# The residual subtractions of a fused attention and MLP kernel: from VectorE or GpSimd to VectorE alone

## The chip, the cores and the metric

One core of a Trainium2 chip. The metric is the device time of one execution in microseconds, the median of the runs shown; three runs of the kernel before are known.

## The reference, cut to what matters

```python
def reference(**kwargs):
    attn_out = _attn_ref(x, a, B, C)                # gated linear attention, 4 x 8 heads, 768 steps, D 32, N 16
    x = attn_out.transpose(0, 2, 1, 3).reshape(3072, 256)
    xn = x / sqrt(mean(x * x) + 1e-6) * rms_g       # MLP 1, d_ff 1536
    g, val = xn @ w_gate, xn @ w_val
    x = (g * sigmoid(g) * val) @ w_out
    h = x @ w_in                                    # MLP 2, d_ff 2048
    return (h * clip(h + 3, 0, 6) / 6) @ w_out2
```

All of it is float32.

## The kernel before, in words

**Two halves for every product.** A matmul operand is split into a high half, rounded to a matmul format (`hi`), and the residual, value minus high half (`lo`). Each product is then three matmuls: high by high, low by high, high by low (`mm3`, its matmuls are all line 752). The residual is one subtraction of two SBUF tiles, and it is issued by `two` (line 248), which takes the engine as an argument. Line 248 also issues two small attention products, `bh` and `ch`. So the tiles written by line 248 are `w1l` and `w2l` (weights), `xl` (a block's input), `gl` (the gated hidden tile), `bh` and `ch`.

**The stages.** Attention works on 24 chunks of 128 positions. A visit to a pair of chunks makes, per chunk, a scan of the decays on VectorE (`L`, line 400), `bh` and `ch`, the scores, the decayed scores (`SM`, line 480), the masked state (`um`), the states (`V`, line 494), and its output. Four chunks make a token block of 512. MLP 1 ("A") runs over 6 blocks with 12 steps each, MLP 2 ("B") over 6 blocks with 16 steps each. The first two pairs of chunks and the block's normalisation come ahead of A; the other chunks and the normalisations of later blocks (`z`, `y`, then `xT`, line 648, then `xh` and `xl`) are woven into the A steps. The weights of MLP 1 are rebuilt in the course of block 0: ScalarE makes two parts, VectorE joins them (line 712), ScalarE or VectorE rounds (`w1h`), and line 248 makes `w1l`.

**A step.** In A: 12 matmuls make two hidden tiles `hps`, ScalarE gates one (`p`, line 785), VectorE multiplies by the other (line 793), ScalarE rounds (`gh`, line 800), line 248 makes `gl`, and 6 matmuls add to `acc`. In B: 6 matmuls, ScalarE (line 787), VectorE (line 795), `gh`, `gl`, 6 matmuls. That makes 72 steps of 18 and 96 steps of 12 matmuls of 512 columns, 2448 in all. The hidden tiles lie in 2 PSUM buffers in A (4 from the middle of the last block but one on, and in B); `p`, `gh` and `gl` have 3 buffers each.

**What sets the order.** Nothing is ordered by hand. Every operation is handed to a planner (`Plan.op`) with the engines that may run it and what it is thought to cost there. At build time `Plan.run` plays the kernel through, gives each operation to one engine, and emits all instructions in the order of its start times; on the chip each engine then works through its list in order. Where an operation has two engines, the planner takes the one that would be done first, with 600 ns (`BIAS`) held against VectorE. While GpSimd runs something, the planner charges VectorE with 0.45 of its time (`SHARE`). `either(n)` (lines 244 and 245) hands over such a pair. It serves `bh` and `ch`, the `xl` of the first half of block 0 (the other half's is VectorE's by its own line) and of all later blocks, `w1l`, `w2l` and `gl`. By the planner's numbers a 512-column subtraction is 604 ns on VectorE (`d1`) and 1313 ns on GpSimd (`g1`), 0.45 of which is 591 ns.

Of the kernel before, what the change touches and what calls it, by code (L numbers as in the profile page):

```python
# [186 lines left out]
def block_kernel(ctx, tc, comb, ablk, w1, w2, cst, out):  # L187
# [44 lines left out]
    def d1(n):  # L232
        return 72 + 1.04 * n
# [7 lines left out]
    def g1(n):  # L241
        return 110 + 2.35 * n

    def either(n):
        return {"DVE": d1(n), "POOL": g1(n)}

    def two(e, out, a, b, op):
        eng[e].tensor_tensor(out=out, in0=a, in1=b, op=op)  # L248
# [92 lines left out]
    def load(q):  # L341
# [71 lines left out]
        for i, k in enumerate((k0, k0 + 1)):  # L413
            P.op({"DVE": ds(512)}, lambda e, k=k: scan(e, k), r=[("eye", 0), Ls[i]], w=[Ls[i]],
                 boost=bst)
            P.op(either(128), lambda e, k=k: bh(e, k), r=[cbs[i], Ls[i]], w=[("bh", k)], boost=bst)
            P.op(either(64 if k < B else 128), lambda e, k=k: ch(e, k), r=[cbs[i], ("P", q)],
                 w=[("ch", k)], boost=bst)
# [138 lines left out]
    def norm_pair(q, b):  # L557
# [44 lines left out]
        def lo(e):  # L602
# [3 lines left out]
        x = [("xT", 0, k0, t) for t in range(2)]  # L606
        P.op({"ACT": a1(512), "DVE": d2(512)}, hi, r=x, w=[("x", b, q, 0)], boost=bst)
        P.op({"DVE": d1(512)} if q else either(512), lo, r=x + [("x", b, q, 0)],
             w=[("x", b, q, 1)], boost=bst)

# [377 lines left out]
```

## Time and profile before

| | us |
|---|---|
| median of 3 runs (lowest, highest) | 643.24 (642.71, 643.81) |
| the profiled execution, its own time | 643.43 |
| span of its instructions | 641.6 |
| PE busy | 608.3 (95%) |
| PEld busy | 491.9 (77%) |
| DVE busy | 311.2 (49%) |
| ACT busy | 293.9 (46%) |
| POOL busy | 282.1 (44%) |

PE is TensorE's matmul, PEld its weight load, DVE VectorE, ACT ScalarE, POOL GpSimd. The span runs from the first to the last instruction. Busy times of PE overlap because matmuls are pipelined, so a window in which PE is shown as busy throughout can still hold fewer matmuls than it could.

### The profile page before, as it was taken

To read this page: it belongs to the slowest core of one execution; us is meant where nothing else is said; L and a number is where in the kernel's file an instruction comes from. 1 tells how busy PE (TensorE), PEld (TensorE's weight loads), DVE (VectorE), ACT (ScalarE), POOL (GpSimd) and SP (SyncE) were. 2 spreads that over 40 slices of the span, in tenths; PEclk is the share of its full clock that TensorE was granted. 3 is DMA by queue.
4 is the path that set the end of the run, shared out by engine and by line. 5 is a ranking of instruction groups with operands and counts; after the bars stand their busy time and mean duration, and the time that the engine had idled before them with its cause. 6 is when DMAs were issued, how large, how long until landed. Compare 5 with 4: busy or idle time off the path is not lost.

```text
span 641.6 us, 10828 instructions
## 1 busy us (share of the span) xinstructions
PE 608.3 (95%) x4414; PEld 491.9 (77%) x4414; DVE 311.2 (49%) x474; ACT 293.9 (46%) x484; POOL 282.1 (44%) x245
## 2 busy tenths in 40 slices
PE   1689999999999999999999999999999999999997
PEld 0567777778777777777888878788788787888886
DVE  4589975771683366255666422422424224222223
ACT  1368743232323233335766344545454454545443
POOL 3255373353334235233544344545455454544443
PEclk9999999999999999999999999999999999999999
DMA  7977314300340220022433000000000000000000
GB/s 254 313 241 287 102 32 129 105 18 1 100 111 7 79 79 17 3 83 76 140 131 113 0 1 0 1 33 2 1 34 1 0 34 1 5 29 1 33 1 33
DMA packets 15817, 42.18 MB, mean 66 GB/s; under 512 B 2116, under 2 KB 5400, under 8 KB 15768
## 3 DMA queue, kind: packets, MB, share of 16 engines
q1 hardware_dynamic: 15064, 39.63, 19.3%
q10 hardware_dynamic: 704, 1.87, 0.8%
q8 instruction: 34, 0.56, 0.4%
q14 instruction: 15, 0.12, 0.1%
HBM read 38.14 MB, written 3.35 MB: 65 GB/s over the span
## 4 chain that ended last, share of the span: by engine, by line
PE 78%; DVE 11%; DMA 5%; issue 4%; SPq 1%; ACT 0%; POOL 0%; DVEq 0%; POOLq 0%
PE hps L752 43%; PE acc L752 31%; DMA rb<-rnd 2%; DVE p L793 1%; DVE z L551 1%; DVE xT L648 1%; PE sps L451 1%; PE sps L460 1%; DVE xl L248 1%; DVE xh L254 1%; DVE yT L712 1%; DMA pref<-ac 1%; PE sps L426 1%; DVE y L552 1%; DMA rnd<-y 1%
## 5 line engine op out<-in xcount | busy, mean ns | idle before, releaser
L248 POOL TENSOR_TENSOR gl<-p,gh 128x512 fp32r<-128x512 f32 x161 | 215.5, 1338 | 300.0 <-ACT gh L800 279.7
L800 ACT CAST gh<-p 128x512 fp32r<-128x512 f32 x168 | 104.7, 623 | 117.2 <-PE acc L752 115.2
L795 DVE SCALAR_TENSOR_TENSOR p<-p,hps 128x512 f32<-128x512 f32 x96 | 65.9, 687 | 175.9 <-ACT p L787 175.8
L787 ACT ACTIVATE p<-hps,half 128x512 f32<-128x512 f32 x96 | 66.0, 687 | 76.9 <-POOL gl L248 76.2
L752 PE MATMUL hps<-xh,w1h 128*128 128x512 f32 x288 | 91.2, 398 | 4.4 <-DVE p L793 3.7
L752 PE MATMUL hps<-xh,w1l 128*128 128x512 f32 x288 | 89.4, 392 | 0.0
L752 PE MATMUL hps<-xl,w1h 128*128 128x512 f32 x288 | 89.2, 391 | 0.0
L793 DVE TENSOR_TENSOR p<-p,hps 128x512 f32<-128x512 f32 x72 | 49.1, 681 | 64.7 <-PE hps L752 56.3
L785 ACT ACTIVATE p<-hps 128x512 f32<-128x512 f32 x72 | 43.0, 598 | 79.4 <-POOL gl L248 66.2
L752 PE MATMUL acc<-gh,w2h 128*128 128x512 f32 x192 | 74.7, 389 | 0.0
L752 PE MATMUL acc<-gl,w2h 128*128 128x512 f32 x192 | 74.7, 389 | 0.0
L752 PE MATMUL acc<-gh,w2l 128*128 128x512 f32 x192 | 74.7, 389 | 0.0
L752 PEld LDWEIGHTS hps<-xh,w1h 128*128 128x128 f32 x288 | 53.1, 190 | 19.2 <-DVE p L793 6.8
L752 PEld LDWEIGHTS hps<-xh,w1l 128*128 128x128 f32 x288 | 54.4, 189 | 11.7
L752 PEld LDWEIGHTS hps<-xl,w1h 128*128 128x128 f32 x288 | 54.4, 189 | 11.6
L752 PE MATMUL hps<-xh,w2h 128*128 128x512 f32 x192 | 59.7, 392 | 2.1 <-DVE p L795 2.1
L752 PE MATMUL hps<-xh,w2l 128*128 128x512 f32 x192 | 59.2, 389 | 0.0
L752 PE MATMUL hps<-xl,w2h 128*128 128x512 f32 x192 | 59.1, 389 | 0.0
L752 PE MATMUL acc<-gh,w1h 128*128 128x512 f32 x144 | 57.4, 399 | 0.9 <-issue 0.9
L752 PE MATMUL acc<-gh,w1l 128*128 128x512 f32 x144 | 56.1, 390 | 0.0
L752 PE MATMUL acc<-gl,w1h 128*128 128x512 f32 x144 | 56.1, 390 | 0.0
L752 PEld LDWEIGHTS hps<-xh,w2h 128*128 128x128 f32 x192 | 35.6, 188 | 11.3 <-DVE p L795 4.3
(98 smaller groups left out, 710.4 us busy)
## 6 DMA issues: line engine op xcount, KB each, us to landing
cb<-comb SPq DMA_DIRECT2D x10, 896.0 KB
raw<-w SPq DMA_DIRECT2D x16, 512.0 KB
L<-azero SPq DMA_DIRECT2D x22, 256.0 KB
yT<-w SPq DMA_DIRECT2D x6, 768.0 KB
rawx<-w SPq DMA_DIRECT2D x6, 768.0 KB
out<-yT SPq DMA_DIRECT2D x12, 256.0 KB
P<-pref SPq DMA_DIRECT2D x24, 64.0 KB
rb<-rnd SPq DMA_DIRECT2D x5, 256.0 KB
```

The lines of the kernel that those rows point to most:

```text
L248: eng[e].tensor_tensor(out=out, in0=a, in1=b, op=op)
L254: dve.tensor_copy(out, a)
L426: pe.matmul(out=o[64 * c:64 * c + 64, p], lhsT=cb[r, BN + c * SC:BN + (c + 1) * SC], rhs=cb[r, CP + c * CH:CP + (c + 1) * CH], start=True, ...
L451: pe.matmul(out=y[32 * g:32 * g + 32, 2 * t + c], rhs=SM[r, h], lhsT=cb[r, XX + D * h:XX + D * h + D], start=first, stop=True, skip_group_ ...
L460: pe.matmul(out=y[q:q + 64, p // 2 * 2 + c], lhsT=before(k, c)[r, :], rhs=T["ch", k][r, SC * c:SC * c + SC], start=False, stop=True, skip_ ...
L551: dve.tensor_tensor(out=z, in0=z, in1=y, op=ALU.mult)
L752: pe.matmul(out=o, lhsT=a, rhs=c, start=first and i == 0, stop=last and i == len(seq) - 1)
L785: act.activation(out=p[:, :n], in_=hid(hs[0])[:, :n], func=AF.Silu)
L787: act.activation(out=p[:, :n], in_=hid(hs[0])[:, :n], func=AF.Relu, scale=1.0 / 6.0, bias=half)
L793: dve.tensor_tensor(out=p, in0=p, in1=h, op=ALU.mult)
L795: dve.scalar_tensor_tensor(out=p, in0=p, scalar=1.0, in1=h, op0=ALU.min, op1=ALU.mult)
L800: act.copy(out=t[:, :n], in_=T["p", i][:, :n])
```

## The change

`either` names VectorE alone. All operations handed over through it therefore run on VectorE, GpSimd keeps only the fills and masks of the setup, and the planner makes a new order for all engines.

```diff
     def either(n):
-        return {"DVE": d1(n), "POOL": g1(n)}
+        return {"DVE": d1(n)}
```

## Rows read from the trace of the kernel before

**Rows 1.** Windows: us, busy us (instructions) by engine, clock, DMA share, GB/s.
```profile
37.00:97.00 60.00, 57.85 (x613) 45.32 (x613) 55.11 (x77) 38.91 (x62) 33.55 (x29) 1.00 0.47 160
...
100.00:300.00 200.00, 195.79 (x2000) 155.88 (x1999) 109.10 (x185) 65.05 (x120) 76.40 (x72) 1.00 0.20 60
...
364.00:641.60 277.60, 271.71 (x1193) 223.07 (x1191) 86.28 (x118) 133.93 (x207) 131.56 (x102) 1.00 0.03 12
```
**Rows 2.** The chain that ended last: start us, us, what.
```profile
444.12 2.72 PE acc L752 x12
```
**Rows 3.** Waits of PE: us in total, times, longest us.
```profile
PE hps L752 <- DVE p L793: 3.7, 7, 0.8
...
PE hps L752 <- DVE p L795: 2.1, 5, 0.7
```
**Rows 4.** POOL by form, window 37 to 97: busy us, mean ns, idle before.
```profile
L248 POOL TENSOR_TENSOR gl<-p,gh 128x512 fp32r<-128x512 f32 x11 | 16.8, 1531 | 19.2 <-ACT gh L800 13.8 <-DVE w1l L248 5.5
L248 POOL TENSOR_TENSOR w1l<-yT,w1h 128x768 fp32r<-128x768 f32 x3 | 6.5, 2151 | 1.8 <-ACT w1h L252 1.8
L248 POOL TENSOR_TENSOR bh<-cb,L 128x128 f32<-128x128 f32 x8 | 5.8, 729 | 5.9 <-DVE L L400 5.9
L248 POOL TENSOR_TENSOR ch<-cb,P 128x128 f32<-128x128 f32 x6 | 3.3, 574 | 0.0
L248 POOL TENSOR_TENSOR xl<-xT,xh 128x512 fp32r<-128x512 f32 x1 | 1.7, 1747 | 0.0
```
**Rows 5.** DVE by tile, whole span: count, least/median/most ns, first and last start.
```profile
L248 DVE TENSOR_TENSOR gl<-p,gh x7: 679/802/1705, 298.8 to 632.9; 128x512 fp32r<-128x512 f32 x7
L248 DVE TENSOR_TENSOR w1l<-yT,w1h x7: 929/950/1945, 39.5 to 81.3; 128x768 fp32r<-128x768 f32 x7
L551 DVE TENSOR_TENSOR z<-z,y x17: 160/293/1269, 26.8 to 278.2; 128x128 f32<-128x128 f32 x15, 128x2 f32<-128x2 f32 x2
L400 DVE TENSOR_TENSOR_SCAN L<-L,eye x24: 1193/1214/2893, 9.8 to 230.5; 128x512 f32<-128x512 f32 x24
L494 DVE SCALAR_TENSOR_TENSOR V<-V,P,um x36: 270/277/1342, 49.5 to 269.4; 128x64 f32<-128x64 f32 x36
L648 DVE SCALAR_TENSOR_TENSOR xT<-xT,gs,rb x10: 739/1040/1777, 84.4 to 286.3; 128x512 f32<-128x512 f32 x10
```
**Rows 6.** DVE by form, window 37 to 97, columns as in rows 4.
```profile
L400 DVE TENSOR_TENSOR_SCAN L<-L,eye 128x512 f32<-128x512 f32 x7 | 12.0, 1747 | 0.0
L248 DVE TENSOR_TENSOR w1l<-yT,w1h 128x768 fp32r<-128x768 f32 x7 | 7.6, 1090 | 0.0
L494 DVE SCALAR_TENSOR_TENSOR V<-V,P,um 128x64 f32<-128x64 f32 x11 | 5.0, 495 | 0.0
L648 DVE SCALAR_TENSOR_TENSOR xT<-xT,gs,rb 128x512 f32<-128x512 f32 x2 | 3.1, 1582 | 1.3 <-DMA rb<-rnd 1.3
L551 DVE TENSOR_TENSOR z<-z,y 128x128 f32<-128x128 f32 x3 | 1.9, 617 | 0.1
```
**Rows 7.** Timeline 17.7 to 24.4: start us, us, instruction [idle before].
```profile
17.80 2.34 DVE L400 TENSOR_TENSOR_SCAN L<-L,eye 128x512 f32<-128x512 f32 x2 [1.13 <-DMA L<-azero]
20.87 1.81 POOL L248 TENSOR_TENSOR w1l<-yT,w1h 128x768 fp32r<-128x768 f32 x1 [6.11 <-ACT w1h L252]
22.64 0.78 POOL L248 TENSOR_TENSOR bh<-cb,L 128x128 f32<-128x128 f32 x2
21.06 1.16 PE L426 MATMUL sps<-cb 32*64 32x128 f32 x32
23.51 0.68 PE L437 MATMUL sps<-cb,bh 64*32 64x64 f32 x32 [1.30 <-POOL bh L248]
```
**Rows 8.** Timeline 405 to 412, the change from one block of B to the next.
```profile
406.33 1.14 DVE L254 CAST xh<-yT 128x512 fp32r<-128x512 f32 x1 [0.41 <-PE hps L752]
407.57 1.60 DVE L248 TENSOR_TENSOR xl<-yT,xh 128x512 fp32r<-128x512 f32 x1
409.10 0.67 DVE L795 SCALAR_TENSOR_TENSOR p<-p,hps 128x512 f32<-128x512 f32 x1
409.08 0.39 PE L752 MATMUL acc<-gl,w2h 128*128 128x512 f32 x1
409.82 0.73 PE L752 MATMUL hps<-xh,w2h 128*128 128x512 f32 x2 [0.36 <-DVE p L795]
```

## The prediction

> **What bounds the kernel now.** I read the windows first, then the chain that ended last, then the waits of PE, and last the two engines that the change touches. The windows show three regimes [rows 1]. From 364 us to the end (MLP 2) PE is busy nearly all the time and VectorE for 86.28 of 277.6 us. The chain there is made of runs of matmuls such as 12 in 2.72 us [rows 2], that is 0.227 us each; the 2448 matmuls of the two MLPs at this pitch are 555 us of the 641.6 us span. No change on VectorE can shorten that part. From 100 to 300 us VectorE has room too, 109.10 of 200 us busy. Block 0 of MLP 1, from 37 to 97 us, is different: VectorE is busy 55.11 of 60 us while GpSimd is busy 33.55 us. There VectorE and PE are about equally near their limit, and this is the place that decides the sign. Outside the pitch, PE waits little for the hidden tiles: 7 waits of 3.7 us in total in MLP 1 and 5 of 2.1 us in MLP 2, all released by VectorE's product `p` [rows 3].
>
> **What VectorE takes on.** The moved operations cost, alone on VectorE: `gl` and `xl` 0.68 us (the least of `gl` there), `w1l` 0.95 us (its median), and `bh` and `ch` about 0.29 us; the last two do not occur there at 128 columns, and the nearest row is another product of two SBUF tiles of that size, median 0.293 us [rows 5]. I take no gain and no loss around it: bounds are the 0.28 us of a still smaller product of two tiles (`V`, median) and the 0.41 us that GpSimd needs for one (0.78 us for two) [rows 5, 7]. In block 0 that is 11 x 0.68 + 3 x 0.95 + 14 x 0.29 + 0.68 = 15.1 us of new VectorE work for the 29 operations of [rows 4].
>
> **What VectorE gets back.** Its own two-input instructions are drawn out while GpSimd works. In block 0 the 7 scans average 1.747 us against a median of 1.214, the 11 states `V` 0.495 against 0.277, the 2 scalings `xT` 1.582 against a least of 0.739, the 3 `z` 0.617 against 0.293, the 7 `w1l` 1.090 against 0.950 [rows 5, 6]. That is 3.7 + 2.4 + 1.7 + 1.0 + 1.0 = 9.8 us that should vanish with GpSimd quiet. Bounds: 0, if the long ones have another cause, and 15.1 us, if the planner's order leaves fewer collisions to begin with than it now has; I take 9.8, since `gl`, `z` and `V` all fall back to one tight least value.
>
> Here the Trainium skill can be weighed against the rows. Its page "SBUF — State Buffer", section "SBUF: two separate sides", says that VectorE's second port pair is shared with GpSimd under an exclusive lock, and that whoever starts first holds it for its whole instruction. The trace agrees in kind: a scan of 2.893 us is the 1.193 of one alone plus 1.700 [rows 5], about as long as one GpSimd instruction here [rows 4]. By that rule as it stands, each of the 7 scans of block 0 would wait for a whole `gl` of some 1.5 us, 10.7 us from the scans alone where the rows give 3.7, and block 0 would come out shorter, not longer; the sum goes by the rows.
>
> **Block 0.** Net, VectorE gets 15.1 - 9.8 = 5.3 us more: 60.4 us of work in a stretch of 60. It is then the bound, by 0.4 us, and 1.3 us of its idle time is a wait for a DMA that no engine shortens [rows 6]. So +1.7 us. The ends: -1.3 us (the DMA wait is covered and some attention work slides into the 91 us that VectorE has free between 100 and 300 us [rows 1]) and +15.1 us with no relief at all.
>
> **The start.** The operation `bh` of the second pair of chunks stands behind `w1l` on GpSimd: its scans end at 20.14 us (17.80 + 2.34), `w1l` runs from 20.87 to 22.68, `bh` only then, and PE, done with the scores at 22.22, idles 1.30 us for it [rows 7]. On VectorE `bh` can follow the scans at once, 0.6 us for both, and be ready before the scores. VectorE's own queue there gets `w1l` as well, 0.95 us, of which the gap to the next work hides most. I take the whole 1.3 us off the start of block 0; bounds 0, if `w1l` or `ch` is put ahead of it in the new order, and -2 us, if the two-input work next to it (drawn out in the same way) shortens too.
>
> **Block changes.** At a change of block in MLP 2 VectorE rounds a half of the next input (1.14 us), subtracts (1.60 us), and only then multiplies (0.67 us); PE waits for that product, and its next matmul starts 0.74 us after the last one instead of 0.227 [rows 8]. So 0.52 us is lost, and there are 5 such waits [rows 3], of which four repeat this pattern and the first (in the last steps of MLP 1) has another order. With GpSimd quiet the subtraction is 0.68 us, but the other half's subtraction and a `gl` join the queue: 1.60 becomes 0.68 + 0.68 + 0.68. From 406.33 us the present queue is 3.4 us long (1.14 + 1.60 + 0.67). With the rounding at about 0.49 us, an estimate in the proportion in which the subtraction shrinks (1.60 to 0.68, so 1.14 to 0.49), the new one is 3.2 us with the `gl` in it and 2.5 without. Each change of block gives back 0.3 to 0.52 us; I take 0.4, four times, -1.6 us. In MLP 1 four normalisations end in the same queue of scaling, rounding, subtracting and product, with the same waits of half a microsecond [rows 3]; I take 0.3 each, -1.2 us, since the `gl` of a step stands there beside more work. The ends for both together: 0 and -5.8 us (all of [rows 3]).
>
> **Steps in between.** In MLP 2 a step is 2.72 us of PE; VectorE then has a product and a `gl`, 0.67 + 0.68 = 1.35 us. ScalarE, PE and VectorE overlap over several steps, so the shorter `gl` (0.68 against some 1.3 us) brings nothing and the queue costs nothing: PE's matmuls cover both. If that cover went, `p` would come late and its wait would show as the two rows of [rows 3] grown. The end of the kernel is a run of matmuls whose `gl` is ready earlier; nothing there. No DMA moves to another queue: none is issued by GpSimd here.
>
> **Sum.** -1.3 (start) + 1.7 (block 0) - 1.2 (MLP 1) - 1.6 (MLP 2) = -2.4 us. The profiled execution took 643.43 us, 0.2 us over the median of 643.24; so 641.0 against the former and 640.8 against the latter. I say 641.0 us.
>
> **Rivals.**
>
> *VectorE's list becomes the limit of block 0 (slower).* The place is 37 to 97 us. The product of a step stands in one list with `gl`, `bh`, `ch`, scans and joins, in the order that the planner fixed with 0.604 us for a subtraction that takes 0.68; where the head of the list waits, everything waits. The net 5.3 us then all falls on the path, and the gaps of MLP 1 stay: +5.3 - 1.6 = +3.7 us, 647 us, and more if the relief is under 9.8. It decides once VectorE's work in block 0 passes the time of its 216 matmuls and the attention in between, which it does by 0.4 us in my sum; so it is near. Against it speak the relief and the free time after 100 us. Chance 0.3. The Trainium skill points this way: "Perfetto Trace Analysis", section "Optimizing Scalar/DVE Operations", says that with VectorE saturated, handing work to ScalarE or even GpSimd may make sense, the opposite of this change. The windows agree for block 0 alone.
>
> *No change.* What GpSimd did cost VectorE in waiting about what it costs to do it there; the planner sees it so as well, 591 ns charged against 604. Start and block 0 cancel (-1.3 + 1.7), and the gaps of half a microsecond stay because the new order is packed as tightly: 643.2 to 643.6 us. For it speaks that 95% of the time is the pitch of PE. Against it, that the gaps come from stretched VectorE instructions. Chance 0.24. The Trainium skill, in that section of "Perfetto Trace Analysis", adds that, because of the shared port, moving work between GpSimd and VectorE might not help; by that rule this is the outcome.
>
> *All small waits go.* The start gains 1.3 us, block 0 nothing, and all 5.8 us of [rows 3] go: -7.1 us, 636.3 us. This needs VectorE to be ahead at every step, which its 92% in block 0 speaks against. Chance 0.08.
>
> *The change does not do what it says*, because the planner would still choose GpSimd: excluded, as the pair has only one entry left.
>
> **Chances.** The forecast, 639.5 to 642.5 us, has 0.38. A difference of 0.2%, 1.3 us, is about what a measurement of this kernel can tell from no change: faster is below 641.9 us, slower above 644.5. Faster: forecast and the last rival, 0.46; same 0.24; slower 0.30. The range from 637.0 to 648.0 us takes in the forecast, no change and the slower rival to a little past its price; the forecast's own range is 639.5 to 642.5.
>
> **What would show it.** In the changed profile GpSimd's busy time falls to a few us; the most ns of scans and `V` fall to their medians; the first 512-column matmul starts some 1.3 us earlier; block 0 ends within 2 us of 97; the waits of `hps` for `p` shrink. Wrong would be: a VectorE without gaps up to 105 us with growing waits of `hps` in block 0 (the slower rival), or scans that still take 2 us.

## The result: 8 us faster, and the profile after

The changed kernel takes 635.00 us (634.44 to 636.01, 4 runs) against 642.98 us (642.58 to 643.81, 4 runs) beside it: a ratio of 0.9876, 95% interval 0.9859 to 0.9893. The forecast was 641.0 us with a range from 637.0 to 648.0: the sign was right, the size was not. The profiled execution, the fastest of the four, took 634.44 us with a span of 632.3, 9.3 us under the span of before; by the medians the gain is 8.0 us.

The page of the changed kernel, busy us (share) and instructions of each engine:

```profile
PE 604.6 (96%) x4414; PEld 492.4 (78%) x4414; DVE 390.8 (62%) x708; ACT 291.8 (46%) x485; POOL 2.7 (0%) x10
```

GpSimd is idle but for the setup. VectorE ran 234 more instructions (708 against 474), yet its busy time rose only by 79.6 us, from 311.2 to 390.8. The windows of the changed kernel, columns as in [rows 1]:

```profile
37.00:97.00 60.00, 59.18 (x623) 47.28 (x624) 57.57 (x108) 40.04 (x63) 0.00 (x0) 1.00 0.48 162
...
364.00:632.30 268.30, 264.50 (x1167) 218.66 (x1166) 141.51 (x214) 129.72 (x205) 0.00 (x0) 1.00 0.03 12
```

In the window of block 0 VectorE did 108 instructions instead of 77 in only 2.5 us more, and PE did more, too. The same instructions of VectorE as in [rows 5], after the change (count, least/median/most ns):

```profile
L248 DVE TENSOR_TENSOR gl<-p,gh x168: 664/691/694, 44.0 to 624.9; 128x512 fp32r<-128x512 f32 x168
...
L400 DVE TENSOR_TENSOR_SCAN L<-L,eye x24: 1198/1217/1225, 10.0 to 228.6; 128x512 f32<-128x512 f32 x24
...
L494 DVE SCALAR_TENSOR_TENSOR V<-V,P,um x36: 272/278/282, 49.7 to 264.5; 128x64 f32<-128x64 f32 x36
...
L648 DVE SCALAR_TENSOR_TENSOR xT<-xT,gs,rb x10: 743/745/753, 83.4 to 281.0; 128x512 f32<-128x512 f32 x10
```

The long ones are gone: the most of the scans was 2893 ns in [rows 5] and is 1225. And the waits of PE, which had two lines for `hps` behind VectorE's product in [rows 3] (in total 5.8 us, 12 times):

```profile
PE sps L437 <- DVE SM L480: 8.5, 4, 5.5
...
PE hps L752 <- ACT p L785: 0.5, 1, 0.5
```

No wait for a product is left. One for ScalarE remains.

**Where the time came from.** The 512-column matmuls can be counted through a trace: the 1st opens block 0 of MLP 1, each block of MLP 1 has 216 of them, each of MLP 2 has 192. The table gives, for the profiled execution of each kernel, the start of the first one and then the us from that place to the next in the count; "blocks 1-4" is a sum, and the last column lists five blocks one by one. From there to the end of the span it is 47.4 to 47.6 us in all of them. At the pitch of [rows 2] a block of MLP 2 is 43.5 us.

```
                       first   block 0  blocks 1-4   block 5   MLP 2, blocks 0 to 4
before                 37.05     61.09      225.85     48.96   45.17 44.17 44.19 44.18 43.52
changed                38.25     58.68      221.33     48.96   43.52 43.52 43.52 43.52 43.52
old order, VectorE     36.72     58.20      221.87     48.96   44.51 43.52 43.52 43.52 43.52
gl alone moved         37.35     61.05      222.87     48.96   43.52 43.52 43.52 43.52 43.52
all but gl moved       38.51     61.94      222.56     48.96   44.91 43.88 43.87 43.87 43.51
gl of MLP 2 alone      37.13     60.43      225.22     48.96   43.96 43.52 43.52 43.52 43.52
idle GpSimd work       38.35     64.41      225.64     49.09   43.52 43.52 43.52 43.52 43.52
the same, other tile   38.15     62.72      224.24     48.96   43.52 43.52 43.52 43.52 43.52
GpSimd fills           40.16     59.95      221.37     48.96   43.52 43.52 43.52 43.52 43.52
```

So of the 9.3 us, block 0 gives 2.4, blocks 1 to 4 give 4.5, MLP 2 gives 3.6, and the start takes 1.2 back. A second profiled execution of the changed kernel (the last pair of experiments) has 60.15 us in block 0 and 221.42 in blocks 1 to 4, so block 0 is uncertain by more than 1 us and the rest is steady. Start and block 0 together are worth nothing that these profiles can tell: block 0 ends at 98.14 us before, and at 96.93 and 98.74 in the two executions of the changed kernel. The gain lies in blocks 1 to 4 and in MLP 2, 8.1 us.

### The profile page after: what moved, and what is told of

Its sections match the earlier page's. It is cut to its first block, busy times and chain, and to the rows that moved or that the text cites. A ratio compares the mean times of both kernels' runs of the same rounds, so it can differ in the third digit from the quotient of the medians.

```text
span 632.3 us, 10634 instructions
## 1 busy us (share of the span) xinstructions
PE 604.6 (96%) x4414; PEld 492.4 (78%) x4414; DVE 390.8 (62%) x708; ACT 291.8 (46%) x485; POOL 2.7 (0%) x10
## 4 chain that ended last, share of the span: by engine, by line
PE 92%; DVE 4%; DMA 1%; issue 1%; ACT 1%; DVEq 0%; ACTq 0%
PE hps L752 50%; PE acc L752 36%; PE sps L451 1%; PE sps L460 1%; DMA pref<-ac 1%; DVE SM L480 1%; PE sps L437 1%; PE sps L426 1%; PE sps L537 1%; DVE yT L712 1%; ACT sq L521 1%; PE sps L622 0%; DMA ac<-ablk 0%; PE sps L574 0%; DVE w1l L248 0%
## 5 line engine op out<-in xcount | busy, mean ns | idle before, releaser
L248 DVE TENSOR_TENSOR gl<-p,gh 128x512 fp32r<-128x512 f32 x168 | 115.6, 688 | 76.0 <-ACT gh L800 75.8
```

## The experiments

Three theories stood. **Port**: VectorE's own two-input instructions are no longer drawn out by GpSimd. **Latency**: `gl` itself takes 0.69 us instead of 1.29. **Order**: the planner, with other engines to choose from, made a better order.

**Old order, all on VectorE.** The planner still chooses between the two engines, so that the order is as before, but VectorE carries everything out:

```diff
     def two(e, out, a, b, op):
-        eng[e].tensor_tensor(out=out, in0=a, in1=b, op=op)
+        dve.tensor_tensor(out=out, in0=a, in1=b, op=op)
```

> The order of the kernel before on every engine (PE's list is the same as before), but everything that went through line 248 is carried out by VectorE at its place in that order. Port and latency: 634 to 637 us, the gain is there without the new order. Order: 642 to 645 us, or more, as VectorE's list was not made for it.

634.44 us, ratio 0.9875 (0.9858 to 0.9891): the whole gain, with PE's list that of the kernel before. The gain does not need the new order. By stage the two orders differ in ways that nearly cancel: against this run the changed kernel starts its first 512-column matmul 1.5 us later and takes 0.5 us more in block 0, and it saves 1.0 us in the first block of MLP 2 (43.52 against 44.51) and 0.5 in blocks 1 to 4.

**The new order, `gl` on GpSimd.** The other way round:

```diff
-            two(e, t[:, :n], T["p", i][:, :n], T["gh", i][:, :n], ALU.subtract)
+            two("POOL", t[:, :n], T["p", i][:, :n], T["gh", i][:, :n], ALU.subtract)
```

> The order of the changed kernel on every engine, but each of the 168 gl is carried out by GpSimd at its place. Three theories. Port: the gain comes from VectorE's two-input instructions no longer being drawn out by GpSimd; most of it then goes again, 640 to 643 us. Latency: the gain comes from gl taking 0.69 us instead of some 1.3, so that p is free sooner and the gate of ScalarE runs earlier; 640 to 643 us as well, but with VectorE's waits for ScalarE grown and its own instructions at their least values. Order: the gain comes from the planner's new order; 634 to 636 us.

657.32 us, ratio 1.0226 (1.0211 to 1.0242): outside all three. The waits of ScalarE and of PE in this run:

```profile
ACT p L787 <- POOL gl L248: 132.3, 96, 2.0
...
PE hps L752 <- DVE p L795: 10.0, 21, 0.8
```

Every gate of MLP 2 waits for the `gl` that frees its `p` (3 buffers), and PE for the product, 21 times instead of 5 in [rows 3]. This does not part port from latency. It shows that an order laid out for a `gl` of 0.6 us has no room for one of 1.29: MLP 2 costs 46.6 to 47.0 us a block.

**Idle work on GpSimd.** The changed kernel, and GpSimd subtracts each `gh` from itself into a scratch tile (whose own line is left out here):

```diff
             two(e, t[:, :n], T["p", i][:, :n], T["gh", i][:, :n], ALU.subtract)
+            pool.tensor_tensor(out=scr[:, :n], in0=T["gh", i][:, :n], in1=T["gh", i][:, :n],
+                               op=ALU.subtract)
```

> The changed kernel, and beside it GpSimd subtracts each gh from itself into a scratch tile that nobody reads: 168 more GpSimd instructions of 512 columns, at about the places where gl stood there. The result is not touched. Port: VectorE's scans and subtractions are drawn out again and the time goes back to 639 to 643 us. Latency and order: 634 to 636 us, since gl stays short and the order is that of the changed kernel.

644.56 us, ratio 1.0021 (1.0011 to 1.0031): the gain is gone, and a little more, though `gl` runs on VectorE and the order is the changed kernel's. VectorE's `gl` and scans in this run, and GpSimd's idle work (tile view, ns least/median/most):

```profile
L249 DVE TENSOR_TENSOR gl<-p,gh x168: 660/691/1532, 44.7 to 635.6; 128x512 fp32r<-128x512 f32 x168
...
L401 DVE TENSOR_TENSOR_SCAN L<-L,eye x24: 1195/1210/2064, 10.1 to 238.1; 128x512 f32<-128x512 f32 x24
...
L806 POOL TENSOR_TENSOR scr<-gh x168: 1039/1482/2307, 44.2 to 636.7; 128x512 bf16<-128x512 f32 x168
```

The most of `gl` is its least and 0.87 us, that of the scans theirs and 0.87: as if some of them waited for most of a GpSimd instruction. Against the changed row of the stage table the idle work takes 5.7 us in block 0 and 4.3 in blocks 1 to 4, and nothing in MLP 2, which stays at its floor; there it meets no subtraction `xl` (the most of these is 696 ns). But the idle work also keeps `gh` from being written again. Hence two controls. A one-column subtraction of `gh` holds the place in time, and behind it GpSimd reads a weight tile that never changes, or makes two fills that read nothing:

```diff
+            pool.tensor_tensor(out=scr[:, :1], in0=T["gh", i][:, :1], in1=T["gh", i][:, :1],
+                               op=ALU.subtract)
+            pool.tensor_tensor(out=scr, in0=w1h[0][:, :512], in1=w1h[0][:, :512], op=ALU.subtract)
```

> As the run with idle work, but GpSimd's 512-column subtraction reads a weight tile that never changes; a one-column subtraction of gh ahead of it keeps it in its place in time, and gh is free after that one. If the idle work slowed the kernel by holding gh, the time is 634.5 to 636.5 us; if by VectorE's instructions being drawn out, 642.5 to 645.5 us, and gl's most ns is again about twice its least.

641.42 us, ratio 0.9966 (0.9953 to 0.9979): some 6 of the 8 us are lost without `gh` being held, 1 us short of what port expected. `gl` is drawn out again:

```profile
L249 DVE TENSOR_TENSOR gl<-p,gh x168: 659/691/1526, 44.9 to 631.8; 128x512 fp32r<-128x512 f32 x168
```

By stage it is 4.0 us in block 0, 2.9 in blocks 1 to 4, and again nothing in MLP 2. Its idle reads are shorter, median 1042 ns instead of 1482, and the remaining 3.1 us to the run before can be that or the holding of `gh`; this stays open.

```diff
+            pool.memset(scr, 0.0)
+            pool.memset(scr, 1.0)
```

(in place of the second subtraction)

> As the run before it, but in place of the 512-column subtraction GpSimd makes two fills of 512 columns, which read nothing. Port by reads: VectorE's instructions keep their least values and the time is 634.5 to 636.5 us. Port by any access of GpSimd: they are drawn out again, 638 us or more.

635.40 us, ratio 0.9869 (0.9852 to 0.9885): nothing is lost. (The profiled execution is the slowest of its four, 637.48 us; its first 512-column matmul comes 1.9 us late, for a reason not followed up.) The same rows of this run:

```profile
L249 DVE TENSOR_TENSOR gl<-p,gh x168: 665/691/695, 47.1 to 628.1; 128x512 fp32r<-128x512 f32 x168
...
L401 DVE TENSOR_TENSOR_SCAN L<-L,eye x24: 1196/1216/1224, 11.9 to 231.8; 128x512 f32<-128x512 f32 x24
...
L808 POOL MEMSET scr<- x168: 524/524/687, 47.3 to 630.4; 128x512 bf16 x168
```

GpSimd is as busy as it was before the change (280.9 us against 282.1), yet `gl` and the scans are no longer than with GpSimd silent. It is GpSimd's 512-column subtractions that draw VectorE out, and not its being busy. Its one-column subtractions, which read SBUF too (median 635 ns), draw out neither. Fills and subtractions differ in more than reading, so that the reading does it is likely but not shown by itself. The Trainium skill says so in "SBUF — State Buffer", section "SBUF: two separate sides": a VectorE instruction with two SBUF inputs contends only against a GpSimd operation that reads SBUF. The runs agree: 695 ns beside fills, 1532 beside reads.

**The parts.** `gl` alone fixed to VectorE, and its complement:

```diff
-        P.op(either(n), lo, r=[("p", i), ("gh", i)], w=[("gl", i)])
+        P.op(alone(n), lo, r=[("p", i), ("gh", i)], w=[("gl", i)])    # alone: {"DVE": d1(n)}
```

> Only gl is fixed to VectorE; weights, xl, bh and ch still have both engines to choose from, and the planner makes its order for that. Port: GpSimd is left with some 65 instructions, mostly in the first 300 us and at the changes of block; the gain of MLP 2 (the four changes of block) is reduced, the waits at the changes of block partly stay: 636 to 640 us. Latency: 634 to 636 us, all of the gain. Order: open, between 634 and 643 us.

```diff
-        P.op(either(n), lo, r=[("p", i), ("gh", i)], w=[("gl", i)])
+        P.op(pair(n), lo, r=[("p", i), ("gh", i)], w=[("gl", i)])     # pair: both; either: DVE alone
```

> The complement of the run with gl alone: weights, xl, bh and ch are fixed to VectorE, gl has both engines and the planner gives 160 of 168 to GpSimd. If the parts add up, 643.1 less what gl alone left over (636.9 to 634.4, so 2.5 us): 640 to 641 us. By the port theory for every stage, gl goes on drawing VectorE out: 641 to 643 us. By the latency theory for MLP 2, the blocks of MLP 2 keep their 44.2 us from first matmul to first matmul instead of 43.5.

636.93 us (ratio 0.9907, 0.9892 to 0.9921) and 640.99 us (0.9960, 0.9945 to 0.9975): of 8 us, `gl` alone brings some 6 and the rest alone some 2.5. The sum is about right, but partly by luck, since by stage the parts do not add up: `gl` alone gives all of MLP 2, and each part alone about 3 of the 4.5 us of blocks 1 to 4. In block 0 neither part shows a gain alone (61.05 and 61.94 us), in a place that is uncertain by 1.5 us. How much of blocks 1 to 4 is the length of `gl` itself is not separated. A last run moves the `gl` of MLP 2 alone:

```diff
-        P.op(either(n), lo, r=[("p", i), ("gh", i)], w=[("gl", i)])
+        P.op(either(n) if A else {"DVE": d1(n)}, lo, r=[("p", i), ("gh", i)], w=[("gl", i)])
```

> The kernel before, with the gl of MLP 2 alone fixed to VectorE; everything else as before (PE's list is the same as before). Stage sum: MLP 2 had lost some 0.65 us at each of four changes of block and 1.0 us more in the first; if short gl alone cures that, its blocks go to 43.5 us each and the time to 639 to 640 us, with blocks 0 to 4 of MLP 1 unchanged within 1 us. If it took the relief of VectorE's xl by GpSimd's silence as well, the blocks stay above 43.8 us and the time at 641 us or more.

639.68 us, ratio 0.9949 (0.9934 to 0.9964), as expected, with MLP 2 at its floor from the second block on. But it is no clean test: PE's list is that of before, VectorE's is not. From MLP 2 on the planner gave VectorE both roundings `xh` and put the product ahead of `xl`. What is drawn out at a change of block shows in the rows for the rounding `xh` and the subtraction `xl`. In this order: before; old order on VectorE; all but `gl` moved (two rows); this run (two rows).

```profile
L254 DVE CAST xh<-yT x6: 422/1138/1146, 314.3 to 538.9; 128x512 fp32r<-128x512 f32 x6
...
L254 DVE CAST xh<-yT x6: 418/420/427, 307.8 to 529.8; 128x512 fp32r<-128x512 f32 x6
...
L257 DVE CAST xh<-yT x6: 414/1136/1140, 313.3 to 537.0; 128x512 fp32r<-128x512 f32 x6
L251 DVE TENSOR_TENSOR xl<-yT,xh x12: 679/684/693, 314.2 to 538.9; 128x512 fp32r<-128x512 f32 x12
...
L254 DVE CAST xh<-yT x10: 419/422/427, 313.1 to 535.6; 128x512 fp32r<-128x512 f32 x10
L248 DVE TENSOR_TENSOR xl<-yT,xh x6: 1014/1018/1568, 313.7 to 536.7; 128x512 fp32r<-128x512 f32 x6
```

Beside a `gl` on GpSimd the rounding takes 1.14 us instead of 0.42, although it reads one tile only; beside GpSimd's half of `xl` VectorE's half is drawn out. With all but `gl` moved, `xl` is clean and the rounding is still long, and the blocks lie about halfway (43.88). VectorE and ScalarE at such a place of that run:

```profile
405.39 1.14 DVE L257 CAST xh<-yT 128x512 fp32r<-128x512 f32 x1 [0.41 <-PE hps L755]
406.63 1.30 DVE L251 TENSOR_TENSOR xl<-yT,xh 128x512 fp32r<-128x512 f32 x2
407.84 0.68 DVE L798 SCALAR_TENSOR_TENSOR p<-p,hps 128x512 f32<-128x512 f32 x1
...
406.28 0.69 ACT L790 ACTIVATE p<-hps,half 128x512 f32<-128x512 f32 x1 [0.26 <-POOL gl L251]
```

ScalarE's gate, which waits for `gl`, is done at 406.97; the product starts 0.87 us later, behind `xl`. So the length of `gl` on GpSimd is not what comes last there; VectorE's drawn-out queue is. In the old order carried out by VectorE the product stands behind `xl` as before, the rounding takes 0.42 us, and the last four of the blocks shown are at 43.52. The port theory holds in MLP 2 as well.

**Costs.** The planner with VectorE's measured times, first in the changed kernel, then with both engines to choose from and everything carried out by VectorE (the line of `two` as in the first experiment):

```diff
     def d1(n):
-        return 72 + 1.04 * n
+        return 150 + 1.05 * n
```

> The changed kernel with a planner that takes VectorE's measured times (150 + 1.05 n ns, 688 for 512 columns, in place of 72 + 1.04 n, 604). If the new order had nothing to do with the gain, 634 to 636 us; if the 1.5 us by which the first 512-column matmul comes later in the changed kernel than in the old order (38.25 against 36.72 us) is due to costs that are too low, 632.5 to 634 us.

> All on VectorE, in the order that the planner makes with both engines to choose from and with VectorE's measured times (150 + 1.05 n ns). A try for a faster version: the order made with both engines had the earliest start, the one with measured times the shortest blocks 1 to 4. If both combine, 632 to 633.5 us; if order is worth nothing once GpSimd is quiet, 634 to 635.5 us as the other three.

634.98 us (0.9868, 0.9854 to 0.9883), no difference to the changed kernel, though its first 512-column matmul comes at 36.94 us, as early as hoped: block 0 takes 60.76 us there. And 632.88 us (0.9847, 0.9830 to 0.9863). As the second seemed faster than the change, both were run once more on one chip:

> The changed kernel itself, beside the next on the same chip: 634.4 to 636 us as before.

> The order made with both engines to choose from and VectorE's measured times, everything carried out by VectorE. If that order is worth 2 us against the changed kernel, 632.5 to 633.5 us and the two intervals lie apart; if the difference was between chips, within 0.8 us of the changed kernel.

635.40 us (ratio 0.9887, 0.9872 to 0.9901) and 633.50 us (0.9849, 0.9834 to 0.9864): the intervals lie apart. The order made as if GpSimd took part, with these costs, and carried out by VectorE alone beats the changed kernel by 1.9 us. In the profiles of its two runs block 0 takes 58.02 us with the first matmul at 38.33, and 58.99 with the first at 37.31, so that it ends at 96.35 and 96.30, against 96.93 and 98.74 in the changed kernel; blocks 1 to 4 are 220.46 and 221.11 against 221.33 and 221.42. What makes that order better is open.

## Why the prediction was right and wrong, point by point

**Which step failed.** The term for the small waits of PE, at the changes of block and in blocks 1 to 4 of MLP 1, was too small: -2.8 us forecast (-1.2 in MLP 1 and -1.6 in MLP 2), -8.1 measured (-4.5 and -3.6). The end set for it, -5.8 us, was the sum of the idle rows of PE, and a wait costs more than its row. The terms for the start and for block 0 had the wrong sign. Together they were forecast at +0.4 us and came out at -1.2 and +0.6 in two executions; that this is near is luck.

**Bound by PE's pitch: right.** MLP 2 ends at 43.5 us a block, which is 192 times the pitch, and nothing goes below it.

**Relief of VectorE: right in kind, 1.6 us too small for block 0.** The durations of [rows 6] fell to those of undisturbed instructions (in block 0 a scan to 1.211 us, `V` to 0.278, `xT` to 0.745, `z` to 0.292, `w1l` to 0.948), and subtractions on GpSimd raised them again. The sum left out the joins (line 712) and VectorE's own `xl`, whose means in block 0 fell too. The scans gave back 3.8 us, as the rows had it and not 10.7.

**What VectorE takes on, and block 0: wrong, +1.7 us forecast, -2.4 measured (-0.9 in the other execution).** The price of 0.68 us for a `gl` is its duration. VectorE's list in block 0 after the change (start us, us):

```profile
94.90 0.28 DVE L248 TENSOR_TENSOR ch<-cb,P 128x128 f32<-128x128 f32 x1
95.10 0.28 DVE L248 TENSOR_TENSOR bh<-cb,L 128x128 f32<-128x128 f32 x1
95.30 0.28 DVE L494 SCALAR_TENSOR_TENSOR V<-V,P,um 128x64 f32<-128x64 f32 x1
95.50 0.69 DVE L248 TENSOR_TENSOR gl<-p,gh 128x512 fp32r<-128x512 f32 x1
96.10 0.28 DVE L248 TENSOR_TENSOR ch<-cb,P 128x128 f32<-128x128 f32 x1
```

The next instruction starts before the last has ended: 0.60 us after a `gl` of 0.69, 0.20 us after a `ch` of 0.28. The lengths overlap by 0.08 us. Priced by the distance of starts, the 29 operations cost 11 x 0.60 + 3 x 0.87 + 14 x 0.20 + 0.60 = 12.6 us (0.87 as the 0.95 less the overlap), not 15.1; less the relief, 11.4 us with the joins and `xl`, that is 1.2 us net, not 5.3. VectorE was busy for 57.57 of the 60 us, and the slower rival's condition, more work than the stretch holds, was not met. The planner's 604 ns had been the better number for a place in the list, though 691 is the length.

**The start: wrong, -1.3 us forecast, +1.2 measured (+1.5 in the other execution).** Moving `bh` by itself was worth some 0.45 us. In the old order carried out by VectorE, PE's idle time there is 0.85 us instead of 1.30, because it is released by `SM`, and before the change `SM` ended at 23.37, only 0.05 us ahead of `bh`. The row of that run, and `SM` before:

```profile
23.14 0.68 PE L437 MATMUL sps<-cb,bh 64*32 64x64 f32 x32 [0.85 <-DVE SM L480]
...
22.69 0.68 DVE L480 TENSOR_TENSOR SM<-sps,L 128x512 f32<-128x512 f32 x1
```

The new order then took even that. The bound of 0 named the kind of cause (something put ahead of `bh`), but not a loss. The timeline after, to be laid beside [rows 7]:

```profile
18.12 2.33 DVE L400 TENSOR_TENSOR_SCAN L<-L,eye 128x512 f32<-128x512 f32 x2
21.55 0.16 DVE L563 TENSOR_SCALAR v<-sps 128x2 f32<-128x2 f32 x1 [1.09 <-PE sps L537]
21.62 0.95 DVE L712 SCALAR_TENSOR_TENSOR yT<-yT 128x768 int32<-128x768 int32 x1
22.49 0.48 DVE L248 TENSOR_TENSOR bh<-cb,L 128x128 f32<-128x128 f32 x2
...
23.83 0.47 PE L437 MATMUL sps<-cb,bh 64*32 64x64 f32 x16 [1.30 <-DVE SM L480]
25.14 0.47 PE L437 MATMUL sps<-cb,bh 64*32 64x64 f32 x16 [0.84 <-DVE SM L480]
...
31.85 1.01 PE L537 MATMUL sps<-ones,sq 128*128 128x1 f32 x4 [1.00 <-ACT sq L521]
```

The new order puts a norm step and a weight join between the scans and `bh`, and PE idles again, twice for `SM`, and later 1.00 us for ScalarE's `sq`. In the old order carried out by VectorE the first matmul comes at 36.72 us, in the changed order at 38.25 and 38.59: this loss is the order's.

**Block changes and blocks 1 to 4: right in kind, the main error of size.** The text took 0.3 to 0.4 us for each of eight changes of block, and for all waits 5.8 us, the sum of [rows 3], as the end of the range. A wait of PE costs more than its row. In [rows 8] the row says 0.36 us; the matmuls start 0.74 us apart instead of 0.227, and the second of the pair that starts at 409.82 comes only 0.34 us later (the pair takes 0.73, one takes 0.39). That is 0.51 + 0.11 = 0.62 us, and a block of MLP 2 got 0.65 us shorter. The row starts to count where a matmul of 0.39 us ends, 0.16 us after the next one could have started. With 0.27 us more for each of 12 waits, [rows 3] is worth 9 us, not 5.8: that alone carries the rival in which all small waits go from 636.3 to 633.1 us. The changed kernel where VectorE makes the next block's input:

```profile
398.47 0.42 DVE L254 CAST xh<-yT 128x512 fp32r<-128x512 f32 x1
398.99 1.29 DVE L248 TENSOR_TENSOR xl<-yT,xh 128x512 fp32r<-128x512 f32 x2
...
399.63 0.39 PE L752 MATMUL acc<-gl,w2h 128*128 128x512 f32 x1
399.86 0.61 PE L752 MATMUL hps<-xh,w2h 128*128 128x512 f32 x2
```

0.23 us, no gap. In MLP 2 the mechanism was the forecast's: rounding and subtraction fall back to 0.42 and 0.69 us. In the old order carried out by VectorE the queue of rounding, two subtractions and product then takes 2.4 us, the forecast's "2.5 without"; no `gl` stands in it, and the forecast had half reckoned with one. That is four times 0.65, 2.6 us, where it took 1.6. The other 1.0 us is the first of the five waits, which the forecast left out; it stays in the old order (44.51) and goes in the new one. In blocks 1 to 4 only 4 of the 7 waits of MLP 1 lie, 1.8 us in rows and 2.9 with 0.27 each. The rest of the 4.5 us is mostly waits of another kind, which the forecast left out; before the change:

```profile
PE acc L752 <- issue: 0.9, 2, 0.5
PE hps L752 <- ACT p L785: 0.7, 2, 0.4
```

All four lie in blocks 1 to 4; afterwards 0.2 us of the first kind is left there and no row of the second.

**No change, by the rule that moving work between the two engines might not help.** That page of the Trainium skill ("Perfetto Trace Analysis", section "Optimizing Scalar/DVE Operations") says only that it might not; here it did, ratio 0.9876. A reason, argued and not measured by itself: VectorE is held for 0.6 us by a subtraction that takes GpSimd 1.29 us.

**The likeliest rival after the fact** was "all small waits go", at 636.3 us and a chance of 0.08. Its mechanism held, no wait for a product is left, but its number is near partly by luck: the start lost 1.2 us instead of gaining 1.3, and the waits were worth more than 5.8. It was held small because VectorE seemed full in block 0, which its list priced by lengths made worse.

## What to carry to other kernels

Where two engines hinder each other, an engine's busy time is no measure of what more it can take: look for instructions of one form whose most is far over their median, and count what comes back before counting what is added. Price an added instruction by the distance of starts in a dense stretch, not by its length; and price a wait of a pipelined engine by the distance of starts, too, less the pitch, not by the idle time in its row. To part order from execution, keep the planner's choice and change only the engine that carries it out: one run showed that the gain does not need the new order.

## What the runs showed of the hardware that had not been expected

VectorE starts its next instruction some 0.08 us before the one ahead is shown as ended (0.60 us after a start of 0.69, 0.20 after one of 0.28). GpSimd fills, 336 of 0.524 us, leave VectorE's `gl` and scans as they are (most of `gl` 695 ns); GpSimd subtractions of 512 columns (1.04 us and more) stretch a `gl` to 1.53. A rounding of one fp32 tile is stretched as well, from 0.42 to 1.14 us, beside a `gl` on GpSimd. After a gap the first 512-column matmul is followed by the next 0.34 us later instead of 0.227.
